# A linear-attention and MLP kernel: the first y turned by one engine, its transfers on another queue, and GpSimd in program order

## The chip, the cores and the metric

The kernel runs on one core of one Trainium2 chip. The metric is the device time in microseconds. Before the change, three runs took 618.65, 619.02 and 620.98 us, median 619.02 us.

## The reference

Two blocks follow one another. The first is a gated linear recurrence over 768 tokens, for 4 batches and 8 heads of 48 dimensions; the second is an MLP with a quick GELU on the 3072 tokens, with 384 and 2048 columns. The activations are f32; the weights arrive as 64-bit floats and are turned into f32 in the kernel.

```python
f = 1.0 / (1.0 + np.exp(-f_logit))
for t in range(S):
    state = f[:, :, t, :, None] * state + np.einsum('bhd,bhe->bhde', k[:, :, t], v[:, :, t])
    y[:, :, t] = np.einsum('bhd,bhde->bhe', q[:, :, t], state)
x = y.transpose(0, 2, 1, 3).reshape(B * S, H * D)
h = x @ w_in
g = h * (1.0 / (1.0 + np.exp(-1.702 * h)))
out = g @ w_out
```

## The kernel before

**Units.** The 3072 tokens are cut into 12 units of 256 tokens, three to a batch. `attention(n)` returns for unit n a list of parts, and `mlp_blocks` and `mlp_unit` return lists of small pieces of the MLP (a few matmuls each), called the fill. `merge(n, fill, ...)` writes out the parts of unit n one after the other and puts pieces of fill between them, in proportion to a share of each kind of part. So TensorE gets attention and MLP of an earlier unit in turn.

**The attention of a unit.** The gates F are multiplied up over six levels (`begin_gates`, L397, tiles `tot`, on GpSimd; from unit 1 on preceded by `half_up`, L365, also GpSimd). A part of kind W (one level) or V (two levels) computes scores `sc` on TensorE (L406), scales k and q in the tile X on DVE (`promote`, L487 for units 0 to 2, L491 later), copies the k of the next level aside on ACT (`set_aside`, tile Kc, L462), and brings the scores into A by masks on DVE (L435, L455). There is one PSUM buffer for sc. Part T turns k (L549, L550). Part S adds up A times v (L502), forms the state products (L593), loads v of the next unit (`load_v`) and advances the four states of the unit on DVE (L608 to L612, tile st). In units 0 to 2, part Bf turns the next unit's gates, Bq its q, and K its k on TensorE (L350) and ACT (L355); K also sets k of level 0 aside and begins the gates. From unit 3 on these are DVE transposes (L338), with tanh on ACT (L368).

The last part of a unit, called inter here, adds the earlier states to y (L633), copies y from PSUM into yT (L646, eight copies of 48 x 256), and sends yT through six DMAs into xT, the layout in which the MLP reads x (`to_x`, L670 and L675). It is written at the head of the first part of the next unit's merge, ahead of that unit's first scores. In unit 0, four of the eight copies go to DVE, in turn with ACT, and the six DMAs are issued on the ACT queue; in all others ACT copies and the sync queue issues.

**The weights** are converted from 64-bit floats on the way in, pair by pair (16 pairs, w_in and w_out in turn): one ACT pass (L223) and four DVE passes (L225 to L228). `convert()` writes one DVE pass; at the end of a pair it fetches another pair by DMA (L205, three buffers). In merge(n) the passes are dealt over the parts, for unit 0 by an explicit list `deal`, one entry for each of its 12 parts: W0, W1, W2, W3, Bf, W4, Bq, W5, T, T, S, K. Fill that needs weights not yet converted is not taken (`ready`).

**The MLP** of units 0 to 3 is plain (L980 for h, L994 and, for unit 3, L785 for o). From unit 4 on, h and o use block products with fewer matmuls (L883, L905, L785), which need sums of weights and of x: N1 to N7 from w_in (`sums_of_w`, L816 on GpSimd, L820 on DVE), written as chores in merge(4) behind the parts of unit 4; sums in place in w_in (`sums_in_place`, L840 and L842, with D5 and D2 on GpSimd), written in the middle of unit 3's o products; and for each unit E sums of xT (`sums_of_x`, L856, on GpSimd), written behind to_x.

**Order.** Up to merge(3) all engines run in the order in which the code is written. After that only TensorE does; for the other engines and queues a planner orders the instructions, and it may put a later one into a gap between earlier ones.

```python
    ctx.enter_context(tc.manual_schedule(engines={mybir.EngineType.PE}))
    fill_order = ExitStack()
    fill_order.enter_context(tc.manual_schedule())
    ...
    fill_order.close()
```

Of the kernel before, what the change touches and what calls it, by code (L numbers as in the profile page):

```python
# [16 lines left out]
def view(t, offset, dims):  # L17

    a = t[:]
    return bass.AP(a.tensor, a.offset + offset, [list(a.ap[0])] + [list(d) for d in dims])  # L20
# [3 lines left out]
def kernel(  # L24
# [33 lines left out]
    nc = tc.nc  # L58
    B, H, S, D = q.shape
# [5 lines left out]
    U = 256  # L65
    NG = U // G
    NC = U // C
    NU = S // U
    NP = H // 2
    HS = 64  # L70
# [17 lines left out]
    wp = ctx.enter_context(tc.tile_pool(name="wp", bufs=2))  # L88
    mlp = ctx.enter_context(tc.tile_pool(name="mlp", bufs=2))
    ps = ctx.enter_context(tc.tile_pool(name="ps", bufs=1, space=bass.MemoryType.PSUM))  # L90
    ctx.enter_context(tc.manual_schedule(engines={mybir.EngineType.PE}))
    fill_order = ExitStack()
    fill_order.enter_context(tc.manual_schedule())

# [45 lines left out]
    at = [wp.tile([P, n], I32, tag="bits", name=f"at{j}", bufs=PAIRS_AHEAD) for j, n in enumerate((1, NL * 64))]  # L140
# [16 lines left out]
    def query(n, f):  # L157

        return ((2, 3), (4, 5) if n < N_FILL else (0, 5))[n % 2][f]
# [16 lines left out]
    for r in range(NGR):  # L176
        ffs = range(r * FG, (r + 1) * FG)
        for ff in ffs[::2]:
            f = slice(ff * P, (ff + 2) * P)
# [7 lines left out]
    NPC = 2 * FG  # L187
    NOP = 4
    fetched, todo = {}, []
    state = {"fetch": 0, "begin": 0, "done": 0}  # L190

    def fetch_weights(engine=nc.sync):
        n = state["fetch"]
# [38 lines left out]
    def convert():  # L232

        if state["begin"] < len(pairs) and len(todo) <= NOP // 2:
            begin_pair(state["begin"])
            state["begin"] += 1
        if todo and todo[0]:
            todo.pop(0)()
        if todo and todo[0] is None:
            todo.pop(0)  # L240
            state["done"] += 2
            fetch_weights()
# [63 lines left out]
    def rows(h):  # L306
        return slice(h * HS, h * HS + D)
# [4 lines left out]
    def attention(n):  # L312
# [10 lines left out]
        t = {"tms": [F]}  # L323
        parts = []

        def part(kind):
            return lambda fn: parts.append((kind, fn))
# [93 lines left out]
        def columns(h, g):  # L421

            return rows(h ^ g)
# [191 lines left out]
        @part("W")  # L615
        def _():

            py = t["py"]  # L620
            for cs in ((1, 0), (2, 3)):
                for a in range(NP):
                    for c in cs:
                        g, f = CHUNK[c]
                        w = HS
                        if t["before"][c] is None:
                            if not n:
                                continue
                            w = 1
                        for h in range(2):  # L630
                            state = t["before"][c][rows(h), a] if w > 1 else t["ahead"][rows(h), NC - 1, a]
                            x = a * HALF + g * HS
                            nc.tensor.matmul(  # L633
                                py[columns(h, g), g, a, f, :w], lhsT=state, rhs=X[rows(h), query(n, f), x:x + w],
                                start=False, stop=True, skip_group_check=True,
                            )
            yT = att.tile([P, NP, NG, G], F32, tag="kn", name=f"yT_{n}", bufs=1)
            xT = xTs[n] = mlp.tile([P, NK, width(n)], F32, tag="xT", name=f"xT_{n}", bufs=3)
            if width(n) > U:
                nc.gpsimd.memset(xT[:, :, U + 1:], 0.0)  # L640
            for f in (1, 0):
                for g in range(NG):
                    for h in range(2):
                        at, step = (g * HS, 1) if f else (U - 1 - g * HS, -1)
                        copy = nc.vector.tensor_copy if n == 0 and h else nc.scalar.copy
                        copy(view(yT[rows(h)], at, [[U, NP], [step, HS]]), py[columns(h, g), g, :, f, :])  # L646
            to_x(lambda h: (yT[rows(h), :NK], lambda r, d: yT[r:r + d, NK]), xT[:, :, :U], NG)
            if n == NALL - 1:

                pl = ps.tile([P, NP], F32, tag="sc", name="y_last")  # L650
                for a in range(NP):
                    for h in range(2):
                        nc.tensor.matmul(
                            pl[rows(h), a:a + 1], lhsT=last["st"][rows(h), NC - 1, a], rhs=q_end[rows(h), a:a + 1],
                            start=True, stop=True,
                        )
                yl = att.tile([P, NP], F32, tag="q_last", name="yT_last", bufs=1)
                for h in range(2):
                    nc.scalar.copy(yl[rows(h)], pl[rows(h)])
                yl = yl.rearrange("p (a g t) -> p a g t", g=1, t=1)  # L660
                to_x(lambda h: (yl[rows(h), :NK], lambda r, d: yl[r:r + d, NK]), xT[:, :, U:U + 1], 1)
            if n > N_FILL:
                sums_of_x(n)

        def to_x(y, x, ng):

            queue = nc.sync if n else nc.scalar
            for h in range(2):
                most, rest = y(h)
                queue.dma_start(out=x[h * D:(h + 1) * D].rearrange("p c (g t) -> p c g t", g=ng), in_=most)  # L670
                at = 0
                while at < D:
                    c, p = (h * D + at) // DR, (h * D + at) % DR
                    w = min(D - at, DR - p)
                    queue.dma_start(  # L675
                        out=x[D2 + p:D2 + p + w, c].rearrange("p (g t) -> p g t", g=ng), in_=rest(h * HS + at, w)
                    )
                    at += w
# [165 lines left out]
    def sums_of_x(n):  # L844

        w = (width(n) + 1) // 2
        sums = [mlp.tile([P, NK, width(n)], F32, tag="xT", name=f"E_{n}_{i}", bufs=3).rearrange("p c t -> p (c t)")
                for i in range(2)]
        at = iter([sums[i][:, j * w:(j + 1) * w] for i in range(2) for j in range(2 * NK)])
        e = E[n] = {f"b{c}{j}": xTs[n][:, c, j * w:(j + 1) * w] for c in range(NK) for j in range(2)}  # L850

        def by(out, x, op, y):
            e.setdefault(out, None)
            if e[out] is None:
                e[out] = next(at)
            nc.gpsimd.tensor_tensor(e[out], e[x], e[y], op)  # L856

        add, sub = ALU.add, ALU.subtract
        by("E4", "b10", sub, "b00")
        by("E12", "E4", add, "b21")  # L860
        by("E3", "b20", add, "b21")
        by("E10", "b01", add, "b21")
        by("E0", "E10", sub, "b11")
        by("E15", "E12", add, "b11")
        by("E6", "E10", sub, "E15")
        by("E9", "b00", sub, "b21")
        by("E11", "b10", add, "b11")
        by("E11", "E11", add, "E3")
        by("E14", "E4", sub, "b20")
# [89 lines left out]
    def width(n):  # L959

        return U + 2 * (n == NALL - 1)
# [138 lines left out]
    def merge(n, fill, columns, share, pieces=0, hold=0, by=1.0, chores=[], deal=()):  # L1100

        parts = parts_of(n)
        total = sum(share(kind) for kind, _ in parts)
        converting = {"W": 3, "T": 3, "B": 1} if n < N_FILL - 1 else {"W": 3, "V": 4, "S": 3, "T": 1, "B": 1}
        total_ops = sum(converting.get(kind, 0) for kind, _ in parts)
        held = sum(share(kind) for kind, _ in parts[:hold])
        at = at_ops = done = ops = 0
        for kind, fn in parts:  # L1110
            ready = state["done"]
            fn()
            for chore in chores[:3]:
                chore()
            del chores[:3]
            at += share(kind)
            at_ops += converting.get(kind, 0)
            most = pieces * NOP // 2
            n_ops = min(int(most * at_ops / (by * total_ops)), most) - ops
            if deal:  # L1120
                n_ops, deal = deal[0], deal[1:]
            ops += n_ops
            first, n_columns = done, max(0, columns * (at - held) / (total - held) - done)

            def some(end):
                nonlocal done
                while fill and done < end and fill[0][2] <= ready:
                    w, emit, _ = fill.pop(0)
                    emit()
                    done += w  # L1130
            for i in range(n_ops):
                some(first + n_columns * i / n_ops)
                convert()
            some(first + n_columns)

    def steady(kind):
        return {"W": 3, "V": 4, "S": 3, "T": 1, "B": 1, "K": 1}.get(kind, 0)
# [21 lines left out]
    fetch_weights()  # L1159
    fetch_weights()  # L1160
    fill = []
    merge(0, fill, 0, steady, deal=(0, 0, 0, 0, 0, 0, 0, 4, 1, 1, 0, 0))
    fill += mlp_blocks((0, 0)) + mlp_blocks((0, 1))
    merge(1, fill, UNIT // 2 - LAG // 2 - 3 * DM, steady, 12, hold=2)
    fill += mlp_blocks((1, 0), (1, 1)) + mlp_blocks((0, 2), (1, 2))
# [43 lines left out]
```

## Time and profile before

| | |
|---|---|
| median of three runs | 619.02 us |
| the profiled execution: its time, its span | 620.25 us, 618.5 us |
| TensorE busy, share of the span | 593.3 us, 96% |
| DVE, ACT, GpSimd busy | 421.5, 252.0, 121.1 us |
| mean granted TensorE clock | 0.986 |
| DMA moved, mean rate | 58.28 MB, 94 GB/s |

Busy time is an average over the span; the stages have different limits. In the profile, PE is TensorE, PEld its weight loads, DVE VectorE, ACT ScalarE, POOL GpSimd, and SPq and ACTq are the queues on which the sync engine and ScalarE issue DMAs. A row of the timeline has the start in us from the start of the span, the duration, engine, line, operation, out<-in and a count, and in brackets the idle time before it with what ended it.

### The profile page before, as it was taken

The numbers are of one execution on the slowest core, as the hardware profiler recorded it, in microseconds if no ns is written. First come the engines' busy times: TensorE is split into PE (matmuls) and PEld (weight loads), VectorE is DVE, ScalarE is ACT, GpSimd is POOL, SyncE is SP. The second block draws the span as 40 slices with busy tenths as digits, with TensorE's granted clock in tenths as the row PEclk, the third lists the DMA queues.
The fourth block names the chain that finished last, engine by engine and source line by source line (L and its number), as shares of the span: only waits on it lengthen the run. The fifth ranks groups of instructions, "written<-read, shape, count | busy, mean of one in ns | idle before, by whom it ended". The sixth has DMA issues, their size and how long they took to land.

```text
span 618.5 us, 18187 instructions
## 1 busy us (share of the span) xinstructions
PE 593.3 (96%) x7762; PEld 525.3 (85%) x7762; DVE 421.5 (68%) x675; ACT 252.0 (41%) x519; POOL 121.1 (20%) x202
## 2 busy tenths in 40 slices
PE   6859999889999999999999999999999999999997
PEld 5638667657677789999999999999999999999997
DVE  1879977975796666777767678667679666442254
ACT  4525443224232524434544454354264363342330
POOL 3010031820011011411401402402402401401100
PEclk9987999979999999999999999999999999999999
DMA  7655675482034344434453343453251121001000
GB/s 176 184 140 138 172 164 148 115 202 80 3 93 99 85 118 113 92 89 109 110 129 86 82 104 101 122 131 74 71 151 39 43 67 28 28 1 28 26 0 27
DMA packets 83313, 58.28 MB, mean 94 GB/s; under 512 B 33633, under 2 KB 75265, under 8 KB 83233
## 3 DMA queue, kind: packets, MB, share of 16 engines
q1 hardware_dynamic: 82192, 55.55, 35.9%
q10 hardware_dynamic: 1041, 1.57, 1.0%
q8 instruction: 61, 1.00, 0.7%
q14 instruction: 19, 0.16, 0.1%
HBM read 43.98 MB, written 8.39 MB: 85 GB/s over the span
## 4 chain that ended last, share of the span: by engine, by line
PE 88%; DVE 7%; ACT 2%; issue 1%; DMA 1%; ACTq 0%; SPq 0%; DVEq 0%
PE h L883 19%; PE o_Y L785 12%; PE h L980 12%; PE o L994 9%; PE o_Z L785 8%; PE h_p L905 7%; PE sc L406 6%; PE o_X L785 4%; PE o_W L785 4%; PE t L350 2%; PE y L633 2%; PE y L502 2%; PE sc L593 1%; ACT yT L646 1%; DVE X L487 1%
## 5 line engine op out<-in xcount | busy, mean ns | idle before, releaser
L491 DVE TENSOR_TENSOR X<-X,tot 128x1024 f32<-128x1024 f32 x45 | 57.1, 1270 | 56.2 <-PE sc L406 50.3
L980 PE MATMUL h<-xT,w_in 128*128 128x256 f32 x384 | 88.5, 386 | 2.4 <-ACT g L984 1.8
L980 PEld LDWEIGHTS h<-xT,w_in 128*128 128x128 f32 x384 | 72.3, 192 | 14.8 <-ACT g L984 2.0
L462 ACT COPY Kc<-X 128x512 f32<-128x512 f32 x72 | 48.1, 668 | 83.1 <-DVE X L491 54.1
L994 PE MATMUL o<-w_out,g 128*128 128x384 f32 x192 | 68.7, 508 | 2.9 <-DVE w_out L228 2.9
L994 PEld LDWEIGHTS o<-w_out,g 128*128 128x128 f32 x192 | 36.8, 197 | 26.4 <-DVE w_out L228 3.6
L883 PE MATMUL h<-E,w_in 128*128 128x128 f32 (+1 forms) x448 | 58.1, 276 | 0.0
L397 POOL TENSOR_TENSOR tot<-F 128x512 f32<-128x512 f32 x12 | 12.5, 1039 | 229.7 <-DVE st L611 224.1
L883 PEld LDWEIGHTS h<-E,w_in 128*128 128x128 f32 x448 | 54.7, 192 | 1.2
L455 DVE COPY_PREDICATED A<-masks,sc 128x256 f32<-128x256 uint32 (+1 forms) x108 | 51.9, 531 | 0.1
L785 PE MATMUL o_Y<-T,S 128*128 128x192 f32 x288 | 51.6, 329 | 0.0
L899 DVE TENSOR_TENSOR g<-g,h 128x512 f32<-128x512 f32 (+1 forms) x45 | 27.8, 626 | 33.7 <-PE h L883 33.4
L984 ACT ACTIVATE g<-h 128x256 f32<-128x256 f32 x64 | 24.0, 383 | 60.7 <-PE h L980 60.3
L785 PEld LDWEIGHTS o_Y<-T,S 128*128 128x128 f32 x288 | 47.1, 190 | 0.5
L905 PE MATMUL h_p<-xT,w_in 128*128 128x256 f32 (+1 forms) x192 | 46.8, 380 | 0.0
L897 ACT COPY g<-h 128x512 f32<-128x512 f32 (+1 forms) x45 | 24.3, 539 | 44.7 <-PE h L883 44.3
L406 PE MATMUL sc<-X,Kc 48*64 48x64 f32 x1440 | 31.0, 222 | 10.6 <-ACT Kc L462 8.2
L406 PEld LDWEIGHTS sc<-X,Kc 48*64 48x64 f32 x1440 | 26.2, 136 | 17.6 <-ACT Kc L462 10.5
L338 DVE STREAM_TRANSPOSE X<-raw 128x512 f32<-128x512 f32 x36 | 38.0, 1107 | 3.2 <-PE y L633 3.0
L856 POOL TENSOR_TENSOR E<-xT 128x128 f32<-128x128 f32 (+1 forms) x40 | 26.6, 678 | 68.3 <-DMA xT<-yT 36.0
L646 ACT COPY yT<-y 48x256 f32<-48x256 f32 x92 | 33.7, 366 | 11.1 <-PE y L633 8.6
L905 PEld LDWEIGHTS h_p<-xT,w_in 128*128 128x128 f32 x192 | 34.0, 191 | 3.3
(117 smaller groups left out, 1066.6 us busy)
## 6 DMA issues: line engine op xcount, KB each, us to landing
bits<-in_moe_w_out_dram SPq DMA_DIRECT2D x8, 768.0 KB
raw<-in_f_logit_dram SPq DMA_DIRECT2D x48, 96.0 KB
raw<-in_k_dram SPq DMA_DIRECT2D x48, 96.0 KB
raw<-in_q_dram SPq DMA_DIRECT2D x44, 96.0 KB
bits<-in_moe_w_in_dram SPq DMA_DIRECT2D x7, 576.0 KB
k_tok<-z SPq DMA_DIRECT2D x56, 64.0 KB
kt<-k_tok SPq DMA_DIRECT2D x14, 256.0 KB
out_dram<-osb SPq DMA_DIRECT2D x18, 192.0 KB
```

Source lines behind the costliest of these rows:

```text
L338: nc.vector.transpose(view(out, at, [[HALF, NP], [step, R4], [R4 * step, 32]]), by_half[:, j, f].rearrange("p a (j d) -> p (a j) d", j=R4) ...
L406: nc.tensor.matmul(t["sc"][g * HS:(g + 1) * HS, h, a, s, :], lhsT=t["Kc", l][rows(h), x:x + HS], rhs=rhs(h, a, g), start=True, stop=True,)
L455: nc.vector.copy_predicated(out=view(A, at, dims), mask=mask.bitcast(U32), data=got)
L462: nc.scalar.copy(c.rearrange("p (n two m) -> p n two m", two=2, m=m), view(X, KF * SLOT, [[2 * m, SLOT // (2 * m)], [(KR - KF) * SLOT + m, ...
L491: nc.vector.tensor_tensor(x, x, y, ALU.mult)
L646: copy(view(yT[rows(h)], at, [[U, NP], [step, HS]]), py[columns(h, g), g, :, f, :])
L785: nc.tensor.matmul(t[name], lhsT=lhs(f), rhs=rhs(f), start=(new and i == 0), stop=(i == HF - 1), skip_group_check=True,)
L883: nc.tensor.matmul(ph[:, t - group.start], lhsT=WA[a][:, t * P:(t + 1) * P], rhs=E[n][b], start=(i == 0 and t == group.start), stop=(i == ...
L899: nc.vector.tensor_tensor(to, to, ph, ALU.add)
L905: nc.tensor.matmul(ph, lhsT=w_in[:, c, (ROWS * FG + f) * P:(ROWS * FG + f + 1) * P], rhs=xTs[n][:, c, :], start=(c == 0), stop=(c == NK - 1),)
L980: nc.tensor.matmul(ph, lhsT=w_in[:, c, ff * P:(ff + 1) * P], rhs=xTs[n][:, c, :], start=(c == 0), stop=(c == NK - 1))
L994: nc.tensor.matmul(t["po"], lhsT=g[ff // FG][:, ff % FG, tt * P:(tt + 1) * P], rhs=w_out[:, ff, :], start=(ff == ffs[0]), stop=(ff == ffs[ ...
```

## The change

Four edits. In unit 0 ACT makes all eight copies into yT, and in all units the half h is the outer loop, so that the four copies of half 0 come first; the six DMAs of to_x go to the sync queue in unit 0 too. The entries of `deal` move three of the six conversion passes of unit 0 from ahead of part S to behind S (one) and behind K (two). GpSimd joins TensorE in running in program order to the end. And a merge that ends short of its columns of fill hands the rest on to the next.

```diff
-    ctx.enter_context(tc.manual_schedule(engines={mybir.EngineType.PE}))
+    ctx.enter_context(tc.manual_schedule(engines={mybir.EngineType.PE, mybir.EngineType.Pool}))
...
-            for f in (1, 0):
-                for g in range(NG):
-                    for h in range(2):
+            for h in range(2):
+                for f in (1, 0):
+                    for g in range(NG):
                         at, step = (g * HS, 1) if f else (U - 1 - g * HS, -1)
-                        copy = nc.vector.tensor_copy if n == 0 and h else nc.scalar.copy
-                        copy(view(yT[rows(h)], at, [[U, NP], [step, HS]]), py[columns(h, g), g, :, f, :])
+                        nc.scalar.copy(view(yT[rows(h)], at, [[U, NP], [step, HS]]), py[columns(h, g), g, :, f, :])
...
-            queue = nc.sync if n else nc.scalar
...
-                queue.dma_start(out=x[h * D:(h + 1) * D].rearrange("p c (g t) -> p c g t", g=ng), in_=most)
+                nc.sync.dma_start(out=x[h * D:(h + 1) * D].rearrange("p c (g t) -> p c g t", g=ng), in_=most)
...
+        columns += state["behind"]
         for kind, fn in parts:
...
             some(first + n_columns)
+        state["behind"] = max(0, columns - done)
...
-    merge(0, fill, 0, steady, deal=(0, 0, 0, 0, 0, 0, 0, 4, 1, 1, 0, 0))
+    merge(0, fill, 0, steady, deal=(0, 0, 0, 0, 0, 0, 0, 3, 0, 0, 1, 2))
```

More of the change, by code (lines that the diff above doesn't have):

```diff
@@ L189 @@
     fetched, todo = {}, []
-    state = {"fetch": 0, "begin": 0, "done": 0}
+    state = {"fetch": 0, "begin": 0, "done": 0, "behind": 0}
     def fetch_weights(engine=nc.sync):
@@ L674, in to_x @@
                     w = min(D - at, DR - p)
-                    queue.dma_start(
+                    nc.sync.dma_start(
                         out=x[D2 + p:D2 + p + w, c].rearrange("p (g t) -> p g t", g=ng), in_=rest(h * HS + at, w)
```

## The prediction

> **What bounds the kernel now.** I read the page first, then TensorE's waits, then the timelines of the stretch that they point to.
>
> ```profile
> PE 593.3 (96%) x7762; PEld 525.3 (85%) x7762; DVE 421.5 (68%) x675; ACT 252.0 (41%) x519; POOL 121.1 (20%) x202
> PE   6859999889999999999999999999999999999997
> ```
>
> TensorE is busy 96% of 618.5 us, and from slice 10 on (155 us) it is full. A change can gain only where PE stands still or runs slowly, ahead of about 140 us, and a stop later than that is lost outright. PE's waits say where:
>
> ```profile
> PE sc L406 <- ACT Kc L462: 8.2, 2, 6.6
> PE o L994 <- DVE w_out L228: 2.9, 1, 2.9
> PE h L980 <- ACT g L984: 1.8, 1, 1.8
> ```
>
> The columns are us in total, times, longest. The 6.6 us is the step from unit 0 to unit 1. The timelines of ACT and PE there (start, us, engine, line, tile, count, idle before and its releaser):
>
> ```profile
> 37.72 0.36 ACT L646 COPY yT<-y 48x256 f32<-48x256 f32 x1 [1.00 <-PE y L633]
> 38.57 0.37 ACT L646 COPY yT<-y 48x256 f32<-48x256 f32 x1 [0.49 <-DVE yT L646]
> ...
> 40.68 0.60 ACTq L670 DMA_DIRECT2D xT<-yT  x1
> 41.32 1.25 ACTq L675 DMA_DIRECT2D xT<-yT  x2
> 43.00 0.54 ACTq L670 DMA_DIRECT2D xT<-yT  x1
> 43.58 2.36 ACTq L675 DMA_DIRECT2D xT<-yT  x2
> 45.98 0.67 ACT L462 COPY Kc<-X 128x512 f32<-128x512 f32 x1 [5.33 <-DMA xT<-yT]
> ```
>
> ```profile
> 46.70 1.14 PE L406 MATMUL sc<-X,Kc 48*64 48x64 f32 x32 [6.62 <-ACT Kc L462]
> ```
>
> The eight copies alternate between ACT and DVE and wait for each other; then ACT itself issues six DMAs (40.68 to 45.94), and only then comes Kc, for which PE waits. Stretches of the windows view (us, length, then busy of PE, PEld, DVE, ACT, POOL, then PE clock, DMA share, GB/s):
>
> ```profile
> 39.50:42.90 3.40, 0.58 (x2) 0.00 (x0) 2.61 (x5) 0.66 (x2) 0.96 (x4) 1.00 0.52 137
> 42.90:53.10 10.20, 6.40 (x68) 5.68 (x69) 7.74 (x12) 4.36 (x9) 0.86 (x1) 0.50 0.49 106
> 53.10:79.20 26.10, 24.44 (x441) 18.11 (x440) 24.78 (x45) 13.78 (x28) 0.93 (x2) 1.00 0.69 173
> 79.20:118.90 39.70, 39.55 (x332) 28.78 (x332) 33.04 (x45) 13.84 (x31) 17.38 (x15) 1.00 0.54 133
> 128.20:131.60 3.40, 1.43 (x5) 0.55 (x3) 3.26 (x6) 1.18 (x2) 2.15 (x2) 1.00 0.49 109
> 131.60:138.50 6.90, 5.93 (x10) 3.20 (x10) 5.21 (x7) 1.94 (x3) 2.03 (x5) 0.51 0.95 230
> ```
>
> Both stalls are followed by a half clock. From 53 to 79 DVE is the bound (24.8 of 26.1), from 79 to 119 PE (39.55 of 39.7).
>
> [...] a window with PE 42% busy (1.43 of 3.40) is followed by half clock; one at 47% (1.60, 117.9 to 121.3) is not. [...] 5.3 us of ACT, in line ahead of Kc. [...] L487 takes 0.69 us alone and 1.75 us beside the N sums (L816).
>
> **The change part by part.**
>
> *yT and xT of unit 0.* ACT gets eight copies at the 0.378 us of later units (eight in 3.02), no DMA; DVE loses four of 0.43 us. When they start: today 37.72, after y L633, which waits for the states.
>
> *deal.* Ahead of the states DVE has six conversion passes (30.68 to 35.07). Three now come after them: L228 of pair 0 (0.97) directly, L225 and L226 of pair 1 (0.6 each) after K. DVE is free at 32.85, but the states need sc L593, which ends at 33.24, so they start near 33.35 instead of 34.98: 1.6 earlier. y L633 then ends near 36.2 instead of 37.67. But ACT first does the Kc of level 0 (35.88 to 36.72), which PE's transposes set and nothing here moves. So: copies 36.75 to 39.8. DVE: states to 36.1, three passes to 38.25, then L487 x2 (sc L406 is done at 37.5) to 39.55, L435 to 40.15, L227 and L228 of pair 1 to 42.05. Kc of level 1 follows the copies: 39.8 to 40.45, instead of 45.98 to 46.65. PE's keep-up matmuls end at 39.0, so PE waits 1.5 us in place of 6.6, too little for half clock. DVE's next L487 starts at 42.05 instead of 46.75 (4.7), and its wait of 0.46 for sc goes.
>
> *xT by SP.* SP is idle from about 33.3: load_v can go ahead at 27.8, since the fetch of pair 3 now stands behind it. Each half is three DMAs, 1.75 us to issue on SP (0.53 and 1.22). First half 38.3 to 40.05, second 40.05 to 41.8, landing some 1.2 us later (as for unit 4: 257.2, E at 258.45), at 43.0. PE reaches L980 at 43.2 after its 32 transposes (2.0 us), instead of 51.38. What stands behind on SP: the four q loads (37.41 today, then 41.9 to 45.5) and the weights of pair 4 (43.96 today, then 45.5 to 47.5). The q loads are needed near 53. Pair 4 lands near 52, and its L223 is due near 54: it holds, with 2 us.
>
> *Then DVE sets the pace.* Following it pass by pass: Q of level 2 starts at 48.1 instead of 54.48, level 3 at 52.0 instead of 58.29. PE, with 9 us gained, waits some 1.5 us here and 1 there. **6.2 us** are gained at 79 us, and from there PE is the bound.
>
> *The copy order, h outside,* is that of all units: the first half of xT issues after four copies, not seven, so xT lands some 1.2 us sooner. PE waits for xT once (0.6, at 147.5): **0.6 us**. Elsewhere it feeds E sums that run ahead of PE.
>
> *behind* does nothing. Counting each merge's columns (7680, 25728, 33408, then 23040 and 22016), the emitted work reaches the target at each end: shortfalls (1433 after unit 2's W0, 1698 after its S) are made up within the merge. The carry stays 0.
>
> *GpSimd in program order.* The nine L816 sums run today at 105.8 to 120.4. They are written in merge(4), behind unit 4's tot (198 to 202), so they move there. On leaving, they free DVE: L225 1.65 instead of 0.56, three of 1.75 instead of 0.69, L226 1.00, L227 1.55 make 5.3 us by 118. F L338 then starts some 2.9 us earlier (at the end of PE's L994 it waits again), tanh L368 and g L984 too: the stall of **1.8 us** at 118.9 goes. On arriving they hold DVE's L491 in unit 4's first two parts. The slack there is 1.5 us (Kc done at 211.6, sc at 213.1) and 2.7 us. Two L491 at up to 1.06 each on the first chain: bounds 0 and 1 us, taken **0.5**. half_up of unit 5 slips from 202.8 to 210, needed near 250.
>
> The in-place sums L840 (D5, D2), today at 230.26, are written behind the E sums of unit 4 (258.45 to 265.0), so D5 comes after them. E begins 1.2 us earlier, D5 is done near 265.2, and PE's first L883 at 264.63 needs it. Bounds 0 and 2, taken **0.6 us**. half_up of unit 6 slips behind it to 268, needed at 294.
>
> *The second stall* (2.94 at 129.6) I keep: between sc L593 (126.77) and L228 lie eight st steps and two conversions on DVE, beside the same tot L397. Its half clock cost 3.0 us (5.93 busy at half); [...] could go or not.
>
> Sum: -6.2 - 0.6 - 1.8 + 0.5 + 0.6 = -7.5 us. The profiled execution took 620.25 us (span 618.5), 1.2 above the median of 619.02; on it the sum gives 612.75, and on the median **611.5 us**.
>
> **The rivals.** 0.5% (3.1 us) is about what a measurement of this kernel can tell from no change.
>
> *More is gained* (0.19). [...] the half clock there goes too: 3.0 us; D5 in time: 0.6. That gives 608. [...]
>
> *It is given back* (0.19). DVE gets pair 4's weights late (2 us of room, DMA share 0.69), or GpSimd's sums cost what they can: nine by 1.06, less 4.2 of slack, 5.3, and D5 2.0, against 1.1 counted. Either takes off 4 to 6: 616.5, with the time inside the 0.5% or just above it.
>
> *Slower: the clock* (0.11). With DVE the bound, PE's new gaps in unit 1's W parts (40 to 75 us) could fill a window to under 45% busy. My sum leaves at most 1.5 us in 3.4, 56% busy, so not. If they do, PE's 24 us of work there runs at half clock; a spell of 10.2 us costs 5.1, and three of them cost 15.3, less 1.5 of room: +13.8 - 7.5 gives 625. [...]
>
> *It doesn't do what it says*: only in behind, as above, and counted.
>
> **How the numbers follow.** 611.5 has 0.51 (609 to 614.5). Of the 0.19 given back, 0.15 falls within 0.5%, the rest still faster; of the likeliest 0.02 ends within. Faster 0.72, same 0.17, slower 0.11. The range of 8 in 10 takes in the rival above and most of that given back: 606.0 to 618.5.
>
> **What would show it.** ACT's eight L646 from about 36.8 without DVE among them, SPq L670 near 38.3, sc L406 of level 1 near 40.5, no half clock near 43, L980 near 43 to 44; L816 behind tot of unit 4, no L984 wait of 1.8; L840 on POOL behind E, with a wait of PE L883 under 2 us. It is wrong if DVE's level 3 does not come near 52, if PE's L816-era gap stays, or if PE past 200 us stops for more than 3 us.

## The result, and the profile after

Twelve runs of the changed kernel had a median of 619.81 us (618.16 to 622.98), twelve of the kernel before beside them 619.0: a ratio of 1.0016, 95% interval 0.9999 to 1.0033. The forecast of 611.5 us, and its range up to 618.5, are missed: nothing was gained. Single runs of one kernel differ by up to 6.5 us, and in most kernels the longer runs have the lower clock, so the experiments below are judged by their medians. The profiled execution of after took 618.16 us (span 616.4, clock 0.988), the shortest of its twelve; that of before, 620.25 us, was among the longer ones.

The first part of the page of after, PE's busy time and two rows of slices:

```profile
PE 592.9 (96%) x7762; PEld 525.6 (85%) x7762; DVE 415.1 (67%) x671; ACT 253.3 (41%) x523; POOL 120.8 (20%) x202
PE   6888999979999999899999999999999999999997
PEclk9979999989999999989999999999999999999999
```

The page alone nearly hides what happened. The seventeenth slice (247 to 262 us) shows 8 for PE, where before had 9, and PEclk has a third dip in the slice behind it. PE's waits in after name it (columns: us in total, times, longest):

```profile
PE sc L406 <- DVE A L455: 4.6, 4, 2.2
PE sc L406 <- ACT Kc L462: 3.3, 3, 1.6
PE o L992 <- DVE w_out L228: 2.9, 1, 2.9
PE sc L406 <- issue: 2.4, 2, 1.4
...
PE h L978 <- DVE sum L1040: 0.6, 1, 0.6
```

In after, lines below the edited y part are two lower than before: L978 is h (L980), L992 is o (L994), L838 the sums in place (L840), L881 the first h of a block product (L883), L814 the N sums on GpSimd (L816), L854 the E sums (L856). The 6.6 us wait for Kc and the 1.8 us wait for g are gone. But waits for A are up from 0.9 to 4.6 us, and one of 2.2 us and one Kc wait of 1.05 us lie at 261 us, where before had none.

**The first 50 us went largely as worked out.** ACT's timeline in after (start, us, engine, line, tile, count, idle before and its releaser):

```profile
36.36 0.85 ACT L462 COPY Kc<-X 128x512 f32<-128x512 f32 x1
37.11 3.02 ACT L645 COPY yT<-y 48x256 f32<-48x256 f32 x8
40.45 0.67 ACT L462 COPY Kc<-X 128x512 f32<-128x512 f32 x1 [0.32 <-DVE X L487]
```

Eight copies in 3.02 us without DVE among them, no DMA issue, and Kc of level 1 at 40.45 (39.8 in the sum, 45.98 before). PE reaches its scores of level 1 and its first h like this:

```profile
37.26 0.39 PE L406 MATMUL sc<-X,Kc 48*64 48x64 f32 x9 [0.61 <-ACT Kc L462]
39.00 0.92 PE L406 MATMUL sc<-X,Kc 48*64 48x64 f32 x23 [1.36 <-issue]
39.85 2.93 PE L114 MATMUL idle<-masks,ident 128*128 128x384 f32 x4
42.70 1.13 PE L406 MATMUL sc<-X,Kc 48*64 48x64 f32 x32
43.77 2.79 PE L350 MATMUL t<-ident,raw 128*64 128x128 f32 x32
46.48 1.56 PE L978 MATMUL h<-xT,w_in 128*128 128x256 f32 x6
```

The scores of level 1 at 42.70 are 2.2 us behind the 40.5 of the sum: PE lost 0.61 and 1.36 us ahead of and among its scores of level 0, and its keep-up matmuls (L114, which only keep PE busy) then ran at half clock, 2.93 us instead of the 1.56 of before. DVE was late too, by its own queue:

```profile
36.46 1.70 DVE L228 TENSOR_TENSOR w_in<-a,s 128x768 f32<-128x768 f32 x1
38.27 0.78 DVE L225 TENSOR_SCALAR s<-a 128x768 int32<-128x768 int32 x1
39.08 0.64 DVE L226 TENSOR_SCALAR a<-s 128x768 int32<-128x768 int32 x1
39.64 1.42 DVE L487 TENSOR_TENSOR X<-X,F 128x512 f32<-128x512 f32 x2
...
43.44 1.29 DVE L487 TENSOR_TENSOR X<-X,tot 128x512 f32<-128x512 f32 x2
```

The L228 moved behind the states took 1.70 us instead of 0.97: GpSimd's tot (L397, 36.30 to about 41) runs beside it. Both engines take longer: the five later steps of tot took 3.71 us in all, where before they took 2.07. The sum had used such a price for the N sums (L487 in before: 1.75 us beside them, 0.69 alone) but not here. Level 1 starts at 43.44 instead of 42.05, level 3 at 53.93 instead of 52.0. At 79 us the lead is 4.4 us (the L487 of unit 2 that started at 79.00 before starts at 74.64), not 6.2.

**The lead then grew, and was lost in one place.** With the 1.8 us stall gone it is 6.4 us at the end of the stall for w_out (126.15 against 132.57). The half clock behind that stall lasts 3.41 us instead of 6.83, and at PE's first L881 the lead is 7.3 us (257.34 against 264.63). Then GpSimd's, DVE's and PE's timelines in after:

```profile
254.61 0.45 POOL L854 TENSOR_TENSOR E<-E,xT 128x128 f32<-128x128 f32 x1
255.03 2.50 POOL L838 TENSOR_TENSOR w_in<-w_in 128x512 f32<-128x512 f32 x2
```

```profile
249.38 0.73 DVE L728 TENSOR_TENSOR g<-g,S 128x512 f32<-128x512 f32 x1
256.33 1.74 DVE L838 TENSOR_TENSOR w_in<-w_in 128x512 f32<-128x512 f32 x1 [6.23 <-POOL w_in L838]
258.00 2.05 DVE L491 TENSOR_TENSOR X<-X,tot 128x1024 f32<-128x1024 f32 x1
```

```profile
257.34 1.05 PE L881 MATMUL h<-xT,w_in 128*128 128x128 f32 x8
258.23 1.06 PE L881 MATMUL h<-xT,N 128*128 128x128 f32 x8
261.53 0.69 PE L406 MATMUL sc<-Qc,Kc 48*64 48x64 f32 x32 [2.25 <-DVE A L455]
263.27 0.69 PE L406 MATMUL sc<-X,Kc 48*64 48x64 f32 x32 [1.05 <-ACT Kc L462]
263.90 2.07 PE L881 MATMUL h<-E,w_in 128*128 128x128 f32 x8
265.75 1.82 PE L881 MATMUL h<-E,N 128*128 128x128 f32 x8
```

In before, D5 and D2 ran much earlier on GpSimd, and the same L491 waited for PE's scores alone:

```profile
230.26 2.95 POOL L840 TENSOR_TENSOR w_in<-w_in 128x512 f32<-128x512 f32 x2 [26.40 <-PE h L980]
```

```profile
259.86 1.38 DVE L491 TENSOR_TENSOR X<-X,tot 128x1024 f32<-128x1024 f32 x1 [2.46 <-PE sc L406]
```

For PE, D5 was in time in after too: its L881 at 257.34 waited for nothing. But one of DVE's in-place sums is C4 + D5, and the planner had put it into DVE's queue ahead of unit 5's next L491. DVE stood for 6.23 us. The scores for L491 were done at 252.4 us, so it would have come at about 252.6 by before's distance from its scores; it came at 258.00, behind a sum that took 1.74 us. A and Kc were late; PE stood 3.3 us; and its clock was halved for the next 3.41 us, in which two groups of eight L881 took 2.07 and 1.82 us (1.16 and 1.06 in before). The lead after it is 2.1 us (267.41 against 269.49): **5.2 us lost**. The windows of after show clock and busy time (us, length, busy of PE, PEld, DVE, ACT, POOL, PE clock, DMA share, GB/s):

```profile
35.25:38.66 3.41, 1.78 (x65) 1.38 (x62) 3.20 (x6) 3.10 (x9) 2.25 (x2) 1.00 0.42 166
38.66:45.49 6.83, 6.49 (x75) 4.57 (x76) 6.76 (x11) 3.54 (x7) 2.19 (x4) 0.50 0.33 78
260.53:263.94 3.41, 1.36 (x65) 1.19 (x65) 2.77 (x7) 1.80 (x4) 0.00 (x0) 1.00 0.00 0
263.94:267.35 3.41, 3.41 (x20) 3.41 (x17) 3.25 (x5) 0.00 (x0) 0.00 (x0) 0.50 0.43 134
```

Each of these two half clocks follows a window of 3.41 us in which PE was idle for 1.6 or 2.1 us. The spells in the traces last 3.41 and 6.83 us (after), 6.83 and 10.24 (before) or 13.65 (the deal alone), one to four times 3.41. The second spell of after (127.41 to 130.82) begins 81.92 us behind the end of the first and ends 133.12 us ahead of the third, 24 and 39 times its own length.

### The profile page after: what moved, and what is told of

It reads as the page before. It is cut to its first block, busy times and chain, and to the rows that moved or that the text cites. A ratio compares the mean times of both kernels' runs of the same rounds, so it can differ in the third digit from the quotient of the medians.

```text
span 616.4 us, 18198 instructions
## 1 busy us (share of the span) xinstructions
PE 592.9 (96%) x7762; PEld 525.6 (85%) x7762; DVE 415.1 (67%) x671; ACT 253.3 (41%) x523; POOL 120.8 (20%) x202
## 4 chain that ended last, share of the span: by engine, by line
PE 82%; DVE 8%; DMA 2%; issue 2%; ACT 2%; SPq 1%; POOL 1%; DVEq 0%; ACTq 0%; POOLq 0%
PE h L881 19%; PE o_Y L783 11%; PE h L978 10%; PE o L992 8%; PE o_Z L783 7%; PE h_p L903 7%; PE sc L406 5%; PE o_W L783 4%; PE o_X L783 4%; PE y L633 2%; PE t L350 2%; PE y L502 2%; PE sc L593 2%; DVE X L487 1%; DVE A L455 1%
## 5 line engine op out<-in xcount | busy, mean ns | idle before, releaser
L491 DVE TENSOR_TENSOR X<-X,tot 128x1024 f32<-128x1024 f32 x45 | 58.4, 1297 | 52.6 <-PE sc L406 44.0
L978 PE MATMUL h<-xT,w_in 128*128 128x256 f32 x384 | 87.7, 383 | 0.6 <-DVE sum L1040 0.6
L978 PEld LDWEIGHTS h<-xT,w_in 128*128 128x128 f32 x384 | 71.7, 190 | 12.4 <-DVE sum L1040 1.0
L992 PE MATMUL o<-w_out,g 128*128 128x384 f32 x192 | 67.5, 501 | 2.9 <-DVE w_out L228 2.9
L397 POOL TENSOR_TENSOR tot<-F 128x512 f32<-128x512 f32 x12 | 12.5, 1040 | 250.2 <-DVE st L611 244.2
L881 PE MATMUL h<-E,w_in 128*128 128x128 f32 (+1 forms) x448 | 59.0, 279 | 0.0
L992 PEld LDWEIGHTS o<-w_out,g 128*128 128x128 f32 x192 | 36.2, 194 | 25.8 <-DVE w_out L228 3.6
L881 PEld LDWEIGHTS h<-E,w_in 128*128 128x128 f32 x448 | 55.6, 194 | 1.2
L338 DVE STREAM_TRANSPOSE X<-raw 128x512 f32<-128x512 f32 x36 | 37.9, 1102 | 3.2 <-PE y L633 3.0
L645 ACT COPY yT<-y 48x256 f32<-48x256 f32 x96 | 35.1, 366 | 7.8 <-PE y L633 6.6
L881 PE MATMUL h<-E,N 128*128 128x128 f32 (+1 forms) x256 | 35.3, 279 | 0.0
```

Source lines behind the costliest of these rows:

```text
L338: nc.vector.transpose(view(out, at, [[HALF, NP], [step, R4], [R4 * step, 32]]), by_half[:, j, f].rearrange("p a (j d) -> p (a j) d", j=R4) ...
L491: nc.vector.tensor_tensor(x, x, y, ALU.mult)
L645: nc.scalar.copy(view(yT[rows(h)], at, [[U, NP], [step, HS]]), py[columns(h, g), g, :, f, :])
L881: nc.tensor.matmul(ph[:, t - group.start], lhsT=WA[a][:, t * P:(t + 1) * P], rhs=E[n][b], start=(i == 0 and t == group.start), stop=(i == ...
L978: nc.tensor.matmul(ph, lhsT=w_in[:, c, ff * P:(ff + 1) * P], rhs=xTs[n][:, c, :], start=(c == 0), stop=(c == NK - 1))
L992: nc.tensor.matmul(t["po"], lhsT=g[ff // FG][:, ff % FG, tt * P:(tt + 1) * P], rhs=w_out[:, ff, :], start=(ff == ffs[0]), stop=(ff == ffs[ ...
```

## The experiments

The theory (A): the y path gained what was foreseen, less about 2 us, and GpSimd's program order gave it back through DVE's queue behind D5. The rival (B): the early gain was worth nothing in the end, whatever GpSimd does. Later expectations test parts of A: which of the early edits brought the gain, and (C) whether half clock in unit 1 takes what is missing of it. The kernel before ran beside all of them, with medians of 618.75 to 618.95 us; the ratios are taken over all runs and are not exactly the quotients of the medians.

**GpSimd free again, the rest of after kept.**

```diff
-    ctx.enter_context(tc.manual_schedule(engines={mybir.EngineType.PE, mybir.EngineType.Pool}))
+    ctx.enter_context(tc.manual_schedule(engines={mybir.EngineType.PE}))
```

> The changed kernel with one edit undone: GpSimd is again ordered by the planner, the other edits stay. Theory A (program order on GpSimd is what takes the gain back: DVE's sum C4 waits 6.2 us for GpSimd's D5, which now stands behind the E sums of unit 4, and holds L491; PE stops for 3.3 us and then runs at half clock for 3.4): 5.2 us come back, 1.8 us are lost again to the N sums at 105 us, so near 616.4 us. Theory B (the gain is real in the profiled execution only; in most executions half-clock spells elsewhere take it): within 1 us of the changed kernel's 619.8. In the profile under A: D5 and D2 near 225, no DVE wait for GpSimd above 1 us, no half clock near 264.

Measured: 616.83 us (22 runs, 614.3 to 620.8), ratio to before 0.9972 [0.9957, 0.9986]. D5 and D2 run at 227.76 on GpSimd, DVE does not wait for them, and there is no half clock near 264. DVE's L491 at that place, and PE's stall of before, which is back:

```profile
257.36 1.47 DVE L491 TENSOR_TENSOR X<-X,tot 128x1024 f32<-128x1024 f32 x1 [2.46 <-PE sc L406]
```

```profile
PE h L978 <- ACT g L982: 1.8, 1, 1.8
```

So GpSimd's order costs after 3.0 us net (619.81 to 616.83), 1.8 of gain already taken off: some 4.8 gross, near the 5.2 of the theory. The rival's 618.8 or more falls.

**GpSimd in program order alone, in the kernel before** (the inverse of that diff).

> The kernel before with one edit: GpSimd in program order. Theory A: it costs 5.2 us near 265 us and saves the 1.8 us stall at 119: 622.4 us. Theory B: 617 to 619, since only the 1.8 us count. In the profile under A: the same DVE wait of some 6 us for D5, and PE stopped for some 3 us behind it.

Measured: 624.15 us (623.41 to 625.35), 1.0089 [1.0072, 1.0107]: slower by 5.2, where 3.4 were expected of A. DVE's timeline in this kernel:

```profile
261.53 1.74 DVE L840 TENSOR_TENSOR w_in<-w_in 128x512 f32<-128x512 f32 x1 [7.37 <-POOL w_in L840]
263.19 2.05 DVE L491 TENSOR_TENSOR X<-X,tot 128x1024 f32<-128x1024 f32 x1
```

The same hold, 7.37 us here; PE's wait for A is 3.12 us. The stall of 1.8 is gone, so the order costs 7.0 gross here, more than the 5.2 of the theory; the half clock after the hold lasts 6.83 us from 266.64 instead of 3.41. That is 1.7 us more by an estimate: half of the 3.42 us by which the spell is longer, from the clock of 0.50 in the spells of after. The run shows that the hold needs no part of the y path.

**D5 and D2 ahead of the E sums, the rest of after kept.** The two GpSimd operations are taken out of `sums_in_place`, which stands in the middle of unit 3's o products, and written at the end of unit 3's h products, ahead of E of unit 4.

```diff
+    def sums_on_pool():
...
+        nc.gpsimd.tensor_tensor(WA["D5"], WA["a12"], WA["a10"], ALU.subtract)
+        nc.gpsimd.tensor_tensor(WA["D2"], WA["a10"], WA["a11"], ALU.add)
...
         def end():
 
+            sums_on_pool()
```

> The changed kernel with D5 and D2 written earlier: at the end of unit 3's h products, so that in GpSimd's program order they stand behind unit 4's last tot and ahead of the E sums of unit 4. Theory A: the whole 5.2 us come back and the 1.8 stay: 614.6 us. Theory B: 619 or more. In the profile under A: D5 near 242, C4 on DVE without a wait, no half clock near 264.

Measured: 614.56 us (613.38 to 617.61), 0.9938 [0.9914, 0.9961]. DVE's timeline around the same place:

```profile
245.62 1.76 DVE L844 TENSOR_TENSOR w_in<-w_in 128x512 f32<-128x512 f32 x1 [1.32 <-POOL w_in L832]
...
255.27 1.52 DVE L491 TENSOR_TENSOR X<-X,tot 128x1024 f32<-128x1024 f32 x1 [2.17 <-PE sc L406]
```

C4 + D5 still waits 1.32 us for GpSimd, where the expectation had no wait, but long before L491 is due; L491 waits for PE's scores and for nothing else, as in before. The place of two GpSimd operations is worth 5.25 us (619.81 to 614.56). The theory's 614.6 holds; the rival's 619 falls.

**The y path alone, in the kernel before**: eight copies on ACT, half h outside, xT by the sync queue (and the two lines of behind); old deal, old order of GpSimd.

> The kernel before with the y edits alone: ACT makes all eight copies, h outside, the six DMAs of unit 0 on the sync queue; deal and GpSimd as before. Theory A (these edits are the whole early gain; the three passes of deal only change places, since behind the states they run beside the gates on GpSimd, where L228 takes 1.70 us instead of 0.97): as the run with GpSimd free, 616.8 us, within 0.8. Rival (deal brings its own 1.6 us, as the prediction had it): 618.4 us. In the profile under A: DVE's L487 of level 1 near 43, as with deal (43.4).

Measured: 616.35 us (12 runs, 613.47 to 618.91), 0.9956 [0.9934, 0.9978]. All that the early part brings is here: 2.65 us. The kernel with GpSimd free differs from this one by the new deal alone, and took 616.83: the deal adds nothing that can be measured. In this kernel's trace level 1 starts at 42.24, 1.2 us sooner than in after: DVE goes from the states straight to the two L487 of level 0 (2.45 us beside tot), where after has three conversion passes ahead of them. PE has a new wait later, which before has not:

```profile
133.33 1.57 PE L633 MATMUL y<-X,st 48*48 48x64 f32 x64 [1.91 <-DVE X L491]
```

**The deal alone, in the kernel before.**

```diff
-    merge(0, fill, 0, steady, deal=(0, 0, 0, 0, 0, 0, 0, 4, 1, 1, 0, 0))
+    merge(0, fill, 0, steady, deal=(0, 0, 0, 0, 0, 0, 0, 3, 0, 0, 1, 2))
```

> The kernel before with the dealt passes alone. Theory A: ACT's copies in turn with DVE and its six DMAs still hold Kc; it starts at most 1 us earlier, so 618.0 to 619.0 us. Rival (deal shortens the way to the first states by 1.6 us and all of it is kept): 617.3 us.

Measured: 622.7 us (621.7 to 622.84), 1.0046 [1.0028, 1.0064]. Both expectations were wrong: slower. ACT's timeline in this kernel:

```profile
37.83 0.37 ACT L646 COPY yT<-y 48x256 f32<-48x256 f32 x1
40.93 0.37 ACT L646 COPY yT<-y 48x256 f32<-48x256 f32 x1 [2.73 <-DVE yT L646]
...
48.31 0.67 ACT L462 COPY Kc<-X 128x512 f32<-128x512 f32 x1 [5.31 <-DMA xT<-yT]
```

With DVE still making half of the copies, the passes moved behind the states stand in its queue ahead of the first of them (L228, L225, L226, to 40.4), ACT waits 2.73 us, and Kc comes 2.3 us later than before; the half clock there lasts 13.65 us instead of 10.24. So that edit is only bearable with the y edit.

**The pass of the deal in another place**: the kernel with D5 ahead, with four passes ahead of the states again, none directly behind them, and two behind K.

```diff
-    merge(0, fill, 0, steady, deal=(0, 0, 0, 0, 0, 0, 0, 3, 0, 0, 1, 2))
+    merge(0, fill, 0, steady, deal=(0, 0, 0, 0, 0, 0, 0, 4, 0, 0, 0, 2))
```

> As the kernel with the sums ahead, with one pass dealt otherwise: L228 of pair 0 goes from behind the first states to ahead of them, where DVE waits 1 us for the state products. Theory A (the early gain fell short of 6.2 us because that L228 ran beside GpSimd's gates, 1.70 us): 0.7 to 1.7 us less than with the sums ahead, 613 to 614. Rival (the shortfall is PE's own, from half clock and instruction issue): no change, 614.6. In the profile under A: the L487 of level 0 near 38.5, level 3 near 52.5.

Measured: 614.41 us (612.98 to 616.43), 0.9916 [0.9893, 0.9939], the same as 614.56: the 613 to 614 of A is missed, and the rival's number stands. DVE's timeline:

```profile
37.61 1.30 DVE L225 TENSOR_SCALAR s<-a 128x768 int32<-128x768 int32 x1
38.94 0.85 DVE L226 TENSOR_SCALAR a<-s 128x768 int32<-128x768 int32 x1
```

L228 is out of the way, and L225, 0.56 us alone, now takes 1.30. In three kernels different DVE operations on SBUF stand there beside tot, and each time they pay: against their times alone, they take 1.2 us more in after, 1.3 more here, and 1.2 more with the y path alone, where it is the two L487. So this run moves the price and does not remove it, and it can't decide between its theory and its rival. Before paid nothing there: its four copies out of PSUM stood beside tot, and they took 0.43 us as ever.

**Half clock in unit 1.** The trace with D5 ahead shows a spell from 51.41, behind a 3.35 us wait of PE for level 3, and then a wait of DVE for PE (its windows, and DVE's L487 of level 4):

```profile
48.00:51.41 3.41, 1.16 (x6) 0.68 (x4) 3.34 (x5) 1.60 (x3) 0.09 (x1) 1.00 0.95 238
51.41:58.24 6.83, 5.73 (x43) 4.75 (x44) 6.66 (x14) 2.32 (x5) 0.00 (x0) 0.50 0.71 197
```

```profile
61.30 0.69 DVE L487 TENSOR_TENSOR X<-X,tot 128x512 f32<-128x512 f32 x1 [1.82 <-PE sc L406]
```

Four matmuls whose results nobody reads (eight instructions in the trace), written ahead of those scores, should prevent it.

```diff
+                    _, level3 = parts[3]
+                    parts[3] = kind, lambda: (keep_up(4), level3())
```

> As the kernel with the sums ahead, with four more keep-up matmuls (results unused) written in front of level 3's scores of unit 1, where PE waits 3.4 us for DVE and the half clock of 6.8 us follows. Theory C (what is missing of the early gain beyond the 1.9 us on DVE goes into half clock behind PE's new wait): the spell at 51 us goes, mean clock 0.992 or more in most runs, 612.5 to 613.5 us. Rival (DVE is the bound there, so the half clock is hidden behind it): no spell at 51 us, but 614 to 615 us.

Measured: 615.25 us (6 runs, 612.32 to 616.35), 0.9939 [0.9916, 0.9962]. Inconclusive: two of the six runs, the profiled one among them, have a clock of 0.997 and 612.3 to 612.8 us, and in that trace no spell stands at 51 us, only one of 3.41 us at 39.3; the other four stand at 0.989 to 0.991 and 614.9 to 616.4. The median is not better than the 614.56 without the matmuls, and neither theory's number was met.

**Two steps further.** In the kernel with D5 ahead, pair 11 of the weights (counted from 0) is converted earlier, so that the second stall (2.9 us for w_out) has no cause:

```diff
-    merge(2, fill, UNIT + 3 * DM, steady, 10)
+    merge(2, fill, UNIT + 3 * DM, steady, 10, deal=(2, 2, 2, 3, 2, 2, 1, 1, 1, 2, 1, 1))
```

> As the kernel with the sums ahead, and in unit 2's merge two conversion passes of DVE (L227 and L228 of pair 11) are dealt to the part in front of the states instead of behind them, into DVE's idle 3.7 us before the state products. Theory A: the 2.9 us stall at 123 us goes, and the half clock behind it (1.2 us in the profiled execution of the changed kernel, up to 3.0): 609 to 611.5 us. Theory B: only the 2.9 us at most, so 616 or more.

Measured: 613.71 us (612.08 to 616.08), 0.9922 [0.9897, 0.9947]: 0.85 less, within the noise, and between the two expectations, which both missed. The stall is gone and another has taken its place, in PE's timeline:

```profile
131.45 1.36 PE L633 MATMUL y<-X,st 48*48 48x64 f32 x64 [3.45 <-DVE X L491]
```

The two k turns (L338) of unit 3 stand behind the states on DVE, and through ACT's Kc and Qc they set L491. So in the next kernel these turns are written ahead of the states of unit 2:

```diff
-                    parts += [("B", begin), (kind, lambda: (states(), begin_gates())), ("B", begin_k)]
+                    parts += [("B", begin), ("B", begin_k), (kind, lambda: (states(), begin_gates()))]
```

> As the kernel with pair 11 ahead, and in unit 2's merge the part that turns the k of unit 3 (DVE L338, ACT Kc and Qc, DVE L491) is written in front of the states, not behind them. Theory A (with pair 11 ahead the 2.9 us stall turned into PE's wait of 3.5 us at y L633 for that L491): the wait goes and with it most of the half clock behind it: 608.5 to 610.5 us. Rival (the states themselves are the next bound, which now wait for L491): 612.5 to 614.

Measured: 610.82 us (610.35 to 613.94), 0.9856 [0.9834, 0.9877], 0.3 above the range of A and well below the rival's. The 3.45 us wait is gone; in the profiled execution, the longest of its runs, a wait for xT of 2.8 us stands at 139.6 in its stead.

The same with the four idle matmuls of unit 1:

> As the kernel with the k of unit 3 ahead, with the same four keep-up matmuls. Theory C: 608.5 to 609.5 us. Rival: 610 to 611 us.

Measured: **609.47 us** (607.74 to 611.67), 0.985 [0.9829, 0.9871], with clocks of 0.994 to 0.997 in all five runs. That is within C's range. It beats both before and after; against the kernel without the matmuls its interval overlaps, so what the matmuls bring isn't shown.

## Why the prediction was wrong, point by point

The forecast was 8.3 us too low. By the terms of its sum: GpSimd's in-place sums cost 4.6 more than priced (5.2 for 0.6), the early part gave 4.15 less (2.65 for 6.2 + 0.6), and the N sums cost 0.5 less. So two steps failed, of about the same size: in the first the path of the wait was wrong, in the second the term was mis-sized.

- **GpSimd's in-place sums, "Bounds 0 and 2, taken 0.6 us": the first step that failed.** It asked who on PE waits for D5, and the answer was nearly right: PE did not. It did not ask which instruction on DVE waits for D5, and what stands behind that instruction. C4 + D5 does, it had no haste, and L491, which is the bound of that stretch, stood behind it in DVE's queue through the wait of 6.23 us: it was held for 3.9 us after its scores were done (252.4 to 256.33) and 1.7 more by the sum itself. The planner had moved C4 + D5 from 239.25 us in before to behind 250 us, but not behind L491; that it counted on an earlier D5 is argued, not shown. The two kernels with GpSimd's order changed alone (+5.2 in before with the 1.8 gained, 3.0 back out of after with the 1.8 lost) and the one with D5 ahead (-5.25) show it. The rival "given back" had priced GpSimd's sums at "D5 2.0" and so named the place, not the mechanism.
- **yT and xT, "6.2 us are gained at 79 us": the second step that failed.** The steps of ACT and of the sync queue hold (copies 37.11, first DMA at 38.63, Kc 40.45). At 79 us 4.4 us are there. The missing 1.8 is the term **deal**, taken as a gain of 1.6: the states did start near 33.35 (33.77), but the three passes behind them were priced at 0.97, 0.6 and 0.6 and took 1.70, 0.78 and 0.64 beside tot, with another 0.7 for pair 2's L228 beside half_up (1.67 at 47.94). With the old deal the y edits alone have a lead of 4.65 at 79 us (L487 at 74.35), though a half clock of 3.41 us stands in unit 1 of that trace, so the deal brought nothing. Its sign "no half clock near 43" failed too: after has one from 38.66 to 45.49.
- **The lead at 79 us is not the same in every execution.** After, GpSimd free and D5 ahead have the same code up to there, and their traces differ. From the first states to level 3 DVE takes 20.2 us in all three. In the last two PE waited longer for level 3 (2.94 and 3.35 us; 1.47 in after), half clock followed, DVE then waited 0.78 and 1.82 us for PE's scores of level 4, and the L487 of unit 2 comes at 75.97 and 77.42 instead of 74.64. From the first states to that L487 it is 40.9 us in after, 41.8 and 42.8 in these two, and 41.0 and 40.9 in the two traces with the idle matmuls, which have no spell there. So such a spell takes 0.9 to 1.9 us of the lead; how often it comes in unprofiled runs is open, and the medians with the idle matmuls don't settle it.
- **From 79 us to the end** the y edits' 4.65 in the trace become 3.3 by the spans (618.5 and 615.2): PE waits 1.91 us for L491 ahead of y L633 at 133.33, which before doesn't do, and no longer 0.6 for xT. The medians give 2.65; most of that difference is that before's profiled execution is 1.2 above its median and that kernel's 0.7.
- **The copy order, 0.6.** Not gained in after: PE's wait of 0.6 for xT is gone, and one of 0.6 for DVE's sum L1040 stands in its place. With the y path alone neither is there, but PE has waited the 1.91 us before.
- **GpSimd leaving 105 to 120, 1.8.** Right: the stall goes, and it returns when GpSimd is free.
- **The N sums arriving, 0.5.** They came behind tot of unit 4 as foreseen, in two groups at 194.3 and 202.9, with half_up of unit 5 between them (201.90) and not behind them as the prediction had it; PE had no wait there: 0.
- **The second stall.** Right: 2.94 us again. The half clock behind it lasted 3.41 us, half of before's 6.83, a chance that the prediction had left open.
- **behind.** Right: with and without those two lines the built program is the same, instruction for instruction.
- **The clock.** The rival's gaps of PE in unit 1 did occur, in part: 1.47 us ahead of level 3 in after, but 2.94 with GpSimd free and 3.35 with D5 ahead, against "at most 1.5". Its price, three spells of 10.2 us, did not: the spells there last 3.41 and 6.83. Its threshold of 45% busy was an estimate, set between two windows of before (128.20 to 131.60, 42% busy, followed by half clock, and 117.9 to 121.3, 47% busy and idle for 1.80 us, not followed). It is also wrong: 35.25 to 38.66 in after was 52% busy, nearly all of it matmuls of 48 x 64, and idle for 1.63 us, and was followed by 6.83 us at half clock.

## What to carry to other kernels

When an instruction is moved later on one engine, list its readers on every engine, and for each reader what stands behind it in that queue: a sum that nobody hurries for can hold the queue's most urgent work (here L491, for 3.9 us and then the 1.7 of the sum itself). When one engine is taken out of a planner's hands, look at what the planner has put on the other engines behind its results. Price a moved DVE pass by what GpSimd does at its new time, not by its mean in the groups (L228 here: 1.70 us for 0.97); and when a DVE operation that GpSimd did not slow is moved away (here the copies of y, 0.43 us beside tot), ask which one takes its place beside GpSimd.

## What the runs showed of the hardware that was not expected

- L225, a DVE operation with one SBUF input, slows beside tot too: 0.56 us alone, 1.30 in the kernel with the pass moved (beside the N sums in before it took 1.65). The DVE copies of y out of PSUM, which stood beside tot in before, took 0.43 us, as they do behind it in the kernel with the deal alone.
- In these traces spells of half clock followed windows of 3.41 us in which PE shows 1.16 (D5 ahead), 1.36 (after), 1.43 (before) and 1.78 us (after) of busy time, the last nearly all of small matmuls; a window with 1.60 was not followed by one (before, 117.9 to 121.3). Busy time alone does not tell them apart.
- PE lost 0.61 and 1.36 us ahead of two groups of scores at 37 to 39 us in after; for the second the trace names only its own issue. In six traces this gap stands at the same place, behind the ninth of 32 scores, and lasts 0.53 to 1.63 us. What it is stays open.
- Runs of one kernel mostly fall by clock (means): in before 0.986 goes with 620.7 us and 0.992 with 618.1, in the kernel with the y path alone 0.986 with 618.6 and 0.997 with 614.1. With the deal alone there is no such order.
